# Split keys kept in DRAM between two passes, reciprocal sums transposed last, and a second score tile at first

## The chip, the cores and the metric

The kernel runs on one core of one Trainium2 chip. Its engines work side by side, each through a list of instructions of its own, in order: TensorE (PE, with its weight loads PEld), VectorE (DVE), ScalarE (ACT), GpSimd (POOL) and SyncE (SP), which here issues every DMA. The metric is the device time of one execution in microseconds, the median of several runs.

## The reference

Inputs are `q`, `k`, `v` (4 batches, 8 heads, 1152 positions, head size 64) and the weights `w_in` (512 x 2048) and `w_out` (2048 x 512); `q`, `k` and `v` come as float32, the weights as float64. Queries are averaged in pairs, so 576 of them meet 1152 keys:

```python
q_pool = q.reshape(B, H, S // factor, factor, D).mean(axis=3)      # factor = 2
scores = scale * np.matmul(q_pool, k.transpose(0, 1, 3, 2))        # scale = 1 / sqrt(D)
scores = scores - np.max(scores, axis=-1, keepdims=True)
attn = np.exp(scores)
attn = attn / (np.sum(attn, axis=-1, keepdims=True) + 1e-09)
attn_out = np.matmul(attn, v)
x = attn_out.transpose(0, 2, 1, 3).reshape(B * S // 2, H * D)      # 2304 x 512
h = x @ w_in
out = np.maximum(0.01 * h, h) @ w_out                              # 2304 x 512
```

## The kernel before

TensorE multiplies in a rounded float32 format (fp32r), so every operand is split into a rounded part ("hi") and the remainder ("lo"), and products are added up from hi and lo matmuls. Making the splits is work for ScalarE (the cast, hi), VectorE (the subtraction, lo) and GpSimd.

**Units.** Attention is cut into 64 units. A unit is one batch, one head and one of two groups of its 576 queries: group 0 has 256 queries in two tiles of 128, group 1 has 320 in three tiles of 108, 106 and 106. Batches 0 to 2 are worked in two passes: group 0 of all 8 heads, then group 1 of all 8 heads. Batch 3 takes both groups of a head in turn. Heads go in pairs that share a load of keys; a pair in a pass is a segment (`sg`), 28 in all.

**A unit's steps.** `load_q`, `q_sum` (GpSimd), `q_tr` (TensorE transpose) and `q_hi`, `q_lo` prepare the queries. For each pair of heads, `load_k` brings 576 KB of keys, `k_tr` transposes them in three groups of three (L311) into a `t` bank, and `k_hi` (cast on ScalarE) and `k_lo` (L326, subtraction on VectorE) write the split keys `kk`, one tile of 128 x 1152 per head, of which there are four. `qk` computes the scores of a query tile in two parts (L393 to L398) into the score banks, `vmax` (L406, L410) takes the row maximum on VectorE, `exp` (L420) the exponentials and their row sums on ScalarE. `rsum` (L429, L433) adds up the sums and takes reciprocals on VectorE; `r_tr` (L438) transposes them on TensorE, each broadcast over 128 columns, and `r_cp` copies them to `rb`. `tr` (L457) transposes the exponentials by key tile, `e_hi` and `e_lo` (L466) split them, `pvm` (L477) multiplies with the split values `vv`. `norm` adds hi and lo halves, multiplies by `rb`, and `x_out` stores the unit in DRAM.

**The feed-forward part.** The weights arrive as 32 tiles of 64-bit numbers and are converted to float32 by hand (`w_f32`: two VectorE, two ScalarE and one GpSimd instruction a tile, L520 to L536) and split (L545); the 16 tiles of `w_in` go to DRAM and are loaded again for each of nine blocks of 256 tokens (`l1`, L593: 192 matmuls a block; `l2`, L615 to L617: 96). A block can start when every head of its tokens is stored. The last three blocks hold tokens of batch 3 and need its last heads.

**What sets the order.** All instructions are issued in an order that a list scheduler makes when the program is built. A step has a priority (`prio`, by the number of its first query tile, smaller first), an estimated duration on its engine, steps that it needs, and buffers that it takes until other steps are done. At each turn, of the steps that could start earliest, the one with the smallest priority is issued. `AHEAD`, `SOONER`, `TR`, `SPLIT`, `PV`, `WIN`, `WOUT` and `WAHEAD` are constants in these priorities and in how many weight tiles are loaded ahead. The chip runs each engine's list in this order and waits on semaphores; the estimates only made the order.

**PSUM.** The eight banks of 512 columns are given out by name: one score tile `s` (banks 0 and 1) with its second part `s2` (2), three transpose banks `t` (3, 4, 7), one output bank `o` (5), one feed-forward bank `ml` (6). `tr` of a unit stands behind `r_tr` in the order that the scheduler may choose:

```python
tags["s"] = [(None, 0, slots("bank", (0, 1)))]
tags["t"] = [(None, 0, slots("bank", (3,), (4,), (7,)))]
tags["ml"] = [(None, 0, slots("bank", (6,))), ...]
step(tr, u, x, ..., order=[("r_tr", u)] if x == 0 else [("tr", u, x - 1)], ...)
```

## Time and profile before

| | |
|---|---|
| three runs | 1094.15, 1096.42, 1097.43 us; median 1096.42 |
| profiled execution | 1097.69 us, span on the core 1095.9 us |
| TensorE | 997.1 us busy (91%), 6748 matmuls; mean granted clock 0.970 |
| VectorE | 775.8 us (71%), 1625 instructions |
| ScalarE | 689.6 us (63%), 1693 |
| GpSimd | 406.2 us (37%), 402 |
| DMA | 158.55 MB, 145 GB/s mean, 43.8% of the 16 engines' time |

The span is the time from the first to the last instruction in the profiled execution. The busy share of an engine is a mean over stages that have different limits, so the table of the stages (below) says more than this one. A line such as L326 is the line of the kernel above. In a table of stretches, "PE 81.09 (x462)" is 81.09 us in which TensorE was busy, in 462 instructions that started there. Two matmuls overlap in the pipeline, so the time that one adds is the distance of the starts and not its own duration. The granted clock is a share of the full 2.4 GHz.

### The profile page before, as it was taken

The page shows a single profiled execution, that of the slowest core. Times are in us where ns is not written, and L with a number is a line of the kernel's source. Part 1 is how long each engine was busy: PE and PEld are TensorE (multiplying, and loading weights), DVE is VectorE, ACT ScalarE, POOL GpSimd, SP SyncE. Part 2 cuts the span into 40 slices and gives each one's busy share as a digit, 9 for nine tenths or more (in the row PEclk, how much of TensorE's full clock was granted, in tenths as well). Part 3 has the DMA queues.
Part 4 walks back from the last instruction along what each step waited for, and adds up shares of the span by engine and source line. Part 5 has one row for each costly group of instructions (what it writes and reads, how often), then busy time and mean ns, then how long its engine had stood idle before and what let it go on. Part 6 is the DMA issues. An engine that isn't in the chain of part 4 may idle for free.

```text
span 1095.9 us, 19300 instructions
## 1 busy us (share of the span) xinstructions
PE 997.1 (91%) x6748; PEld 906.3 (83%) x6748; DVE 775.8 (71%) x1625; ACT 689.6 (63%) x1693; POOL 406.2 (37%) x402
## 2 busy tenths in 40 slices
PE   5666788988999989999999999999999999799998
PEld 4555677787898979989899989988999888789896
DVE  7898889997788787777788788776778666411110
ACT  6777877877677666667677667776667665311110
POOL 5666557654233243222434242223222231133220
PEclk8788989999999999999999999999999999899999
DMA  8866546252264353524444433524243130286640
GB/s 263 283 213 214 179 141 232 84 210 90 73 203 143 103 161 100 170 79 150 144 157 134 136 129 116 182 66 162 76 136 105 30 125 25 63 293 231 191 164 29
DMA packets 83953, 158.55 MB, mean 145 GB/s; under 512 B 8592, under 2 KB 44944, under 8 KB 83856
## 3 DMA queue, kind: packets, MB, share of 16 engines
q1 hardware_dynamic: 83856, 157.32, 43.8%
q8 instruction: 53, 0.87, 0.3%
q14 instruction: 44, 0.36, 0.1%
HBM read 139.46 MB, written 17.83 MB: 144 GB/s over the span
## 4 chain that ended last, share of the span: by engine, by line
PE 68%; DVE 18%; issue 5%; DMA 4%; ACT 2%; POOL 2%; SPq 0%; DVEq 0%; POOLq 0%; ACTq 0%
PE banks L593 15%; PE banks L457 11%; PE banks L477 11%; PE banks L615 5%; PE banks L617 5%; PE banks L616 5%; DVE mx L406 5%; PE banks L393 4%; PE banks L394 4%; DVE kk L326 3%; DVE et L466 2%; PE banks L397 2%; PE banks L311 2%; PE banks L398 2%; DVE raw L529 2%
## 5 line engine op out<-in xcount | busy, mean ns | idle before, releaser
L466 DVE TENSOR_TENSOR et<-banks,et 128x320 fp32r<-128x320 f32 (+2 forms) x448 | 233.5, 536 | 70.3 <-ACT et L194 66.8
L194 ACT CAST et<-banks 128x320 fp32r<-128x320 f32 (+2 forms) x448 | 201.2, 470 | 120.5 <-PE banks L477 67.0
L406 DVE TENSOR_REDUCE mx<-banks 128x1 f32<-128x768 f32 (+2 forms) x320 | 234.2, 751 | 60.0 <-PE banks L394 49.9
L420 ACT ACTIVATE e<-banks,mx 128x768 f32<-128x768 f32 (+2 forms) x320 | 238.2, 745 | 56.6 <-DVE mx L410 49.8
L477 PE MATMUL banks<-et,vv 128*128 128x320 f32 (+1 forms) x1152 | 245.9, 323 | 5.8 <-DVE mx L410 4.1
L593 PE MATMUL banks<-xb,ws 128*128 128x256 f32 x1728 | 243.9, 286 | 7.8 <-ACT g L601 2.2
L457 PE MATMUL banks<-ident,e 128*128 128x128 f32 (+2 forms) x1440 | 219.2, 275 | 33.7 <-DVE et L466 14.5
L593 PEld LDWEIGHTS banks<-xb,ws 128*128 128x128 f32 x1728 | 224.2, 190 | 15.5 <-ACT g L601 4.8
L457 PEld LDWEIGHTS banks<-ident,e 128*128 128x128 f32 (+2 forms) x1440 | 174.9, 147 | 61.9 <-DVE et L466 21.6
L477 PEld LDWEIGHTS banks<-et,vv 128*128 128x128 f32 x1152 | 171.0, 194 | 10.8 <-DVE mx L410 5.0
L343 POOL TENSOR_TENSOR qs<-qn 80x256 f32<-80x256 f32 (+1 forms) x128 | 78.5, 633 | 195.8 <-PE banks L351 134.0
L606 POOL TENSOR_TENSOR gg<-g,gg 128x512 fp32r<-128x512 f32 x62 | 80.2, 1294 | 178.4 <-DVE gg L194 146.2
L393 PE MATMUL banks<-kk,qq 128*128 128x384 f32 (+2 forms) x320 | 118.1, 369 | 9.3 <-ACT e L420 9.1
L373 POOL TENSOR_TENSOR vv<-vr,vv 128x576 fp32r<-128x576 f32 x56 | 80.2, 1432 | 97.1 <-DVE vv L194 87.7
L394 PE MATMUL banks<-kk,qq 128*128 128x384 f32 (+2 forms) x320 | 111.4, 348 | 1.0 <-DVE qq L357 1.0
L326 DVE TENSOR_TENSOR kk<-banks,kk 64x384 fp32r<-64x384 f32 (+1 forms) x224 | 98.9, 454 | 14.2 <-ACT kk L194 10.0
L601 ACT ACTIVATE g<-banks 128x512 f32<-128x512 f32 x72 | 43.0, 597 | 102.2 <-PE banks L593 101.5
L615 PE MATMUL banks<-wo,gg 128*128 128x512 f32 x248 | 101.9, 411 | 0.9 <-ACT g L601 0.7
L194 ACT CAST kk<-banks 64x384 fp32r<-64x384 f32 (+1 forms) x224 | 83.9, 392 | 23.6 <-PE banks L311 13.7
L617 PE MATMUL banks<-wo,gg 128*128 128x512 f32 x248 | 97.6, 394 | 0.0
L616 PE MATMUL banks<-wo,gg 128*128 128x512 f32 x248 | 97.4, 393 | 0.0
L492 POOL TENSOR_TENSOR xo<-x,rb 64x256 f32<-64x256 f32 (+1 forms) x64 | 53.1, 829 | 71.4 <-DVE x L489 67.3
(60 smaller groups left out, 1275.1 us busy)
## 6 DMA issues: line engine op xcount, KB each, us to landing
ws<-wd SPq DMA_DIRECT2D x144, 512.0 KB, 4.3
vr<-in_v_dram SPq DMA_DIRECT2D x56, 288.0 KB, 3.4
kn<-in_k_dram SPq DMA_DIRECT2D x27, 576.0 KB, 3.9
raw<-in_moe_w_in_dram SPq DMA_DIRECT2D x16, 512.0 KB, 5.4
wd<-ws SPq DMA_DIRECT2D x16, 512.0 KB, 4.1
raw<-in_moe_w_out_dram SPq DMA_DIRECT2D x16, 512.0 KB, 5.0
qn<-in_q_dram SPq DMA_DIRECT2D x32, 160.0 KB, 2.4
out_dram<-raw SPq DMA_DIRECT2D x18, 256.0 KB, 2.0
```

What stands on the lines that cost most here:

```text
L194: ENG[e].copy(out=out, in_=in_) if e == "ACT" else ENG[e].tensor_copy(out=out, in_=in_)
L393: nc.tensor.matmul(p[:, c], lhsT=hi, rhs=key[:, c * CW:(c + 1) * CW], start=True, stop=False)
L394: nc.tensor.matmul(p[:, c], lhsT=lo, rhs=key[:, c * CW:(c + 1) * CW], start=False, stop=True)
L406: nc.vector.tensor_reduce(out=m[:, part:part + 1], in_=sps[u, j, part], axis=(AX.XY, AX.X)[part], op=ALU.max)
L420: nc.scalar.activation(out=d, in_=sps.pop((u, j, part)), func=AF.Exp, bias=mxs[u, j][:n, 2:3], accum_out=st[u][:n, c:c + 1])
L457: nc.tensor.transpose(p[:, a * w + o:a * w + o + n], ex[u, j][:n, t * 128:(t + 1) * 128], ident[:n, :n])
L466: nc.vector.tensor_tensor(out=et[u, x][:, 1, :w], in0=tps.pop((u, x))[:, :w], in1=f32(et[u, x])[:, 0, :w], op=ALU.subtract)
L477: nc.tensor.matmul(p, lhsT=vv[vis_of[u]][:, korder[vis_of[u] % 2][t], :], rhs=et[u, x][:, y, a * w:(a + 1) * w], start=(t == 0 and y == 0) ...
L593: nc.tensor.matmul(p, lhsT=wst[i, f][:, a, c, :], rhs=xx[i][:, x, c, :], start=(n == 0), stop=(n == 3 * KC - 1))
L615: nc.tensor.matmul(p, lhsT=gh, rhs=wo[f][:, 0], start=(f == hf * FH), stop=False)
L616: nc.tensor.matmul(p, lhsT=gh, rhs=wo[f][:, 1], start=False, stop=False)
L617: nc.tensor.matmul(p, lhsT=gl, rhs=wo[f][:, 0], start=False, stop=(f == hf * FH + FH - 1))
```

## The change

Three things change in what the steps do.

1. **Keys kept.** In batches 0 to 2 the first pass saves each head's split keys `kk` to a DRAM buffer (`k_save`, 128 x 1152 float32), and the second pass loads them into a `kk` tile (`k_back`) in place of `load_k`, `k_tr`, `k_hi` and `k_lo`. A `kk` tile of the first pass is free when both its last score matmul and its save are done.
2. **Reciprocal sums.** `r_tr` writes 64 rows from 64 broadcast columns instead of 128, its priority is `p0 + RT` (2.5) instead of `p0 - 1`, and `tr` no longer stands behind it.
3. **Banks.** Until the second part of the sixth unit's second tile has been exponentiated (`early`), banks 6 and 7 hold a second score tile; `ml` gets bank 6 and `t` bank 7 only after that.

Six constants differ too. (The new code also has a path for unsplit operands, `plain`, which is off with `PLAIN = 0` and left out here.)

```diff
+KEEP = True
+RT = 2.5
+EARLY = 5
-AHEAD = 3.0
-SOONER = 4.0
-TR, SPLIT, PV = 1.5, 1.0, 2.0
+AHEAD = 4.0
+SOONER = 5.0
+TR, SPLIT, PV = 1.5, 1.0, 3.0
-WAHEAD = 3
-WIN = (-2.0, 0.8)
-WOUT = (20.0, 1.0)
+WAHEAD = 2
+WIN = (0.0, 0.8)
+WOUT = (18.0, 1.0)
...
+    first_seg = {}
+    for sg, bh in enumerate(seg_bh):
+        first_seg.setdefault(bh, sg)
+    kept = {sg: first_seg[bh] for sg, bh in enumerate(seg_bh) if KEEP and PLAIN <= first_seg[bh] < sg}
...
+    kd = {2 * sg + j: dram.tile([128, S], F32, name=f"kd{2 * sg + j}") for sg in set(kept.values()) for j in range(2)}
...
-    tags["s"] = [(None, 0, slots("bank", (0, 1)))]
+    early = ("exp", EARLY, 1, 0)
+    tags["s"] = [(None, 0, slots("bank", (0, 1))), (None, early, slots("bank", (6, 7)))]
     tags["s2"] = [(None, 0, slots("bank", (2,)))]
-    tags["t"] = [(None, 0, slots("bank", (3,), (4,), (7,)))]
+    tags["t"] = [(None, 0, slots("bank", (3,), (4,))), (early, 0, slots("bank", (7,)))]
     tags["o"] = [(None, 0, slots("bank", (5,)))]
-    tags["ml"] = [(None, 0, slots("bank", (6,))), (tail, 0, slots("bank", (0,), (1,), (2,), (3,), (4,), (7,)))]
+    tags["ml"] = [(early, 0, slots("bank", (6,))), (tail, 0, slots("bank", (0,), (1,), (2,), (3,), (4,), (7,)))]
...
+    def k_save(hd, e):
+        nc.sync.dma_start(out=kd[hd], in_=f32(kk[hd]))
+
+    def k_back(hd, e, i):
+        kk[hd] = new("kk", i)
+        nc.sync.dma_start(out=f32(kk[hd]), in_=kd[2 * kept[hd // 2] + hd % 2])
...
-            nc.tensor.transpose(p[:, o:o + n], st[u][:n, 8 + j:9 + j].to_broadcast([n, 128]), ident[:n, :n])
+            nc.tensor.transpose(p[:64, o:o + n], st[u][:n, 8 + j:9 + j].to_broadcast([n, 64]), ident[:n, :n])
...
+            hold = [("qk", us[-1], len(tiles_of(us[-1])) - 1, 1)] + ([("k_save", hd)] if sg in kept.values() else [])
+            if sg in kept:
+                step(k_back, hd, prio=pr + 0.1, **sp(1, 0.59e6), deps=[("k_save", 2 * kept[sg] + j)],
+                     order=[("k_back", hd - 1) if j or sg - 1 in kept else ("k_tr", sg - 1, NCH - 1)], takes=[("kk", hold)])
...
+            if sg in kept.values():
+                gis = [gi for gi in range(NCH) if any(y[0] == j for y in KPART[gi])]
+                step(k_save, hd, prio=pr, **sp(1, 0.59e6), deps=[("k_lo", sg, gi, x) for gi in gis for x, y in enumerate(KPART[gi]) if y[0] == j])
...
+                if sg in kept:
+                    keys = [("k_back", hd)]
...
-        step(r_tr, u, prio=p0 - 1, eng=trs(*[x[1] for x in tiles_of(u)]), deps=[("rsum", u, 1)], takes=[("t", [("r_cp", u)])])
+        step(r_tr, u, prio=p0 + RT, eng=trs(*[64 for x in tiles_of(u)]), deps=[("rsum", u, 1)], takes=[("t", [("r_cp", u)])])
...
-                 deps=[("exp", u, t, x) for t in range(ntile) for x in range(2)], order=[("r_tr", u)] if x == 0 else [("tr", u, x - 1)], takes=[("t", [("e_lo", u, x)])])
+                 deps=[("exp", u, t, x) for t in range(ntile) for x in range(2)], order=[("tr", u, x - 1)] if x else [("r_tr", u)] if RT < 0 else [], takes=[("t", [("e_hi" if plain(u) else "e_lo", u, x)])])
```

What this does to the order of the instructions is seen at three places. In the changed kernel the score matmuls are L437 to L442, the key transposes L328, the query transposes L378, those of the exponentials L505 and of the sums L486, the value matmuls L531 and the second layer L674 to L676.

TensorE, the start. Before, from the second part of the first score tile on (`kk` and `qq` are the split keys and queries):

```order
L397 MATMUL banks<-kk,qq 128x384
L398 MATMUL banks<-kk,qq 128x384
L393 MATMUL banks<-kk,qq 128x384
L394 MATMUL banks<-kk,qq 128x384
L393 MATMUL banks<-kk,qq 128x384
L394 MATMUL banks<-kk,qq 128x384
L397 MATMUL banks<-kk,qq 128x384
L398 MATMUL banks<-kk,qq 128x384
L351 MATMUL banks<-ident,qs 128x128 x2
L311 MATMUL banks<-ident,kn 128x128 x9
```

Now, from the same matmul on:

```order
L441 MATMUL banks<-kk,qq 128x384
L442 MATMUL banks<-kk,qq 128x384
L437 MATMUL banks<-kk,qq 128x384
L438 MATMUL banks<-kk,qq 128x384
L437 MATMUL banks<-kk,qq 128x384
L438 MATMUL banks<-kk,qq 128x384
L328 MATMUL banks<-ident,kn 128x128 x6
L441 MATMUL banks<-kk,qq 128x384
L442 MATMUL banks<-kk,qq 128x384
L378 MATMUL banks<-ident,qs 128x128 x2
L328 MATMUL banks<-ident,kn 128x128 x3
```

Before, the whole second tile comes ahead of the next transposes of keys (`kn`). Now only its first part, which has banks 6 and 7, does; six key transposes stand between it and its second part.

TensorE, the sums of the 12th unit (batch 0, second pass). Before (`stat` holds the sums, `e` the exponentials, `wo` and `gg` belong to the second layer):

```order
L617 MATMUL banks<-wo,gg 128x512
L438 MATMUL banks<-ident,stat_67 128x108
L438 MATMUL banks<-ident,stat_67 128x106 x2
L393 MATMUL banks<-kk,qq 106x384
L394 MATMUL banks<-kk,qq 106x384
L393 MATMUL banks<-kk,qq 106x384
L394 MATMUL banks<-kk,qq 106x384
L457 MATMUL banks<-ident,e 128x108
L457 MATMUL banks<-ident,e 128x106 x2
L457 MATMUL banks<-ident,e 128x108
```

Now, around the same unit's sums:

```order
L676 MATMUL banks<-wo,gg 128x512
L674 MATMUL banks<-wo,gg 128x512
L675 MATMUL banks<-wo,gg 128x512
L676 MATMUL banks<-wo,gg 128x512
L486 MATMUL banks<-ident,stat_67 64x108
L486 MATMUL banks<-ident,stat_67 64x106 x2
L531 MATMUL banks<-et,vv 128x320 x4
L378 MATMUL banks<-ident,qs 128x80 x4
L531 MATMUL banks<-et,vv 128x320 x2
```

Before, the sums (L438) stand ahead of every transpose of the unit's exponentials. Now they stand behind the last of these, among the last value matmuls.

VectorE, from the 12th unit's sums on. Before (L326 makes the lo half of the keys, L466 that of the exponentials, L357 that of the queries):

```order
L429 SCALAR_TENSOR_TENSOR stat_67<-stat_67 108x3
L410 TENSOR_REDUCE mx<-mx 108x1
L433 RECIPROCAL stat_67<-stat_67 108x3
L194 CAST wo<-raw 128x512
L357 SCALAR_TENSOR_TENSOR qq<-banks,qq 128x320
L326 TENSOR_TENSOR kk<-banks,kk 64x384
L194 CAST wo<-raw 128x512
L326 TENSOR_TENSOR kk<-banks,kk 64x384
L406 TENSOR_REDUCE mx<-banks 106x1 x2
L466 TENSOR_TENSOR et<-banks,et 128x320
L410 TENSOR_REDUCE mx<-mx 106x1
```

Now (L514 is the lo half of the exponentials, L384 that of the queries, L453 and L457 are the maxima, L477 and L481 the sums and reciprocals, L584 and L588 convert weights):

```order
L477 SCALAR_TENSOR_TENSOR stat_67<-stat_67 108x3
L453 TENSOR_REDUCE mx<-banks 108x1
L481 RECIPROCAL stat_67<-stat_67 108x3
L457 TENSOR_REDUCE mx<-mx 108x1
L514 TENSOR_TENSOR et<-banks,et 128x320 x2
L384 SCALAR_TENSOR_TENSOR qq<-banks,qq 128x320
L584 TENSOR_SCALAR raw<-raw 128x512
L200 CAST wo<-raw 128x512
L588 SCALAR_TENSOR_TENSOR raw<-raw 128x512
L453 TENSOR_REDUCE mx<-banks 106x1 x2
L514 TENSOR_TENSOR et<-banks,et 128x320
L457 TENSOR_REDUCE mx<-mx 106x1
```

The key subtractions are gone from this stretch, which belongs to a second pass; subtractions of exponentials and a weight tile have moved up in their place.

On SyncE the 27 loads of 576 KB of keys become 15, and 24 saves and 24 loads back of 576 KB are added.

## Rows read from the trace of the kernel before

**Rows 1.** Busy time by stage: PE, PEld, DVE, ACT, POOL, clock, DMA share, GB/s.
```profile
0.00:20.00 20.00, 11.19 (x40) 8.69 (x40) 12.48 (x24) 13.39 (x29) 7.31 (x17) 1.00 0.80 252
20.00:140.00 120.00, 81.09 (x462) 69.59 (x462) 108.34 (x205) 90.73 (x209) 76.13 (x70) 0.83 0.66 221
140.00:260.00 120.00, 103.00 (x709) 91.61 (x709) 110.34 (x219) 93.29 (x228) 71.77 (x64) 0.97 0.49 166
260.00:920.00 660.00, 639.06 (x4524) 591.59 (x4525) 509.28 (x1108) 457.68 (x1158) 210.44 (x223) 0.99 0.38 122
920.00:960.00 40.00, 33.17 (x206) 29.26 (x205) 20.02 (x44) 17.76 (x43) 6.04 (x5) 0.87 0.18 54
960.00:1096.00 136.00, 129.64 (x812) 115.57 (x810) 15.36 (x31) 16.73 (x29) 34.51 (x25) 1.00 0.54 182
```

**Rows 2.** The profile's groups, VectorE: busy us, mean ns, idle before.
```profile
L326 DVE TENSOR_TENSOR kk<-banks,kk 64x384 fp32r<-64x384 f32 (+1 forms) x224 | 98.9, 454 | 14.2 <-ACT kk L194 10.0
```

**Rows 3.** Key subtractions (L326): stretch, length, DVE busy, clock, DMA share, GB/s.
```profile
140.00:260.00 120.00, 13.67 (x31) 0.97 0.49 166
```

**Rows 4.** Key transposes (L311): PE and PEld busy, else the same.
```profile
260.00:920.00 660.00, 26.00 (x171) 20.79 (x171) 0.99 0.38 122
```

**Rows 5.** TensorE in order of time: start, us, instruction, count, idle before.
```profile
215.32 0.49 PE L311 MATMUL banks<-ident,kn 128*128 128x128 f32 x3
215.56 0.54 PE L477 MATMUL banks<-et,vv 128*128 128x320 f32 x2
...
823.33 0.44 PE L351 MATMUL banks<-ident,qs 80*128 80x80 f32 x4
823.56 0.83 PE L477 MATMUL banks<-et,vv 128*128 128x320 f32 x4
...
834.40 0.82 PE L311 MATMUL banks<-ident,kn 128*128 128x128 f32 x6
834.98 0.42 PE L393 MATMUL banks<-kk,qq 128*128 128x384 f32 x1
```

**Rows 6.** Waits of TensorE, 260 to 920 us: total us, times, longest.
```profile
PE banks L438 <- DVE kk L326: 5.4, 5, 2.5
PE banks L457 <- DVE mx L410: 5.1, 5, 1.7
PE banks L457 <- DVE et L466: 3.4, 3, 1.6
...
PE banks L438 <- DVE stat L433: 1.2, 2, 1.0
```

**Rows 7.** The same, 0 to 140 us.
```profile
PE banks L457 <- DVE et L466: 9.6, 6, 4.1
...
PE banks L457 <- DVE mx L410: 5.1, 4, 1.4
...
PE banks L457 <- DVE kk L326: 3.0, 2, 2.4
```

**Rows 8.** TensorE in order of time, the start.
```profile
12.62 0.69 PE L393 MATMUL banks<-kk,qq 128*128 128x384 f32 x1 [2.49 <-ACT e L420]
...
22.78 0.69 PE L393 MATMUL banks<-kk,qq 128*128 128x384 f32 x1 [3.58 <-ACT e L420]
```

**Rows 9.** TensorE in order of time, the last unit.
```profile
940.59 0.80 PE L438 MATMUL banks<-ident,stat 108*128 108x108 f32 x3 [2.70 <-DVE stat L433]
```

**Rows 10.** DMA issues: count, KB each, median us to landing.
```profile
kn<-in_k_dram SPq DMA_DIRECT2D x27, 576.0 KB, 3.9
...
wd<-ws SPq DMA_DIRECT2D x16, 512.0 KB, 4.1
```

**Rows 11.** Transposes of the reciprocal sums (L438): columns as in rows 4.
```profile
140.00:260.00 120.00, 3.43 (x21) 2.00 (x21) 0.97 0.49 166
```

**Rows 12.** Weight loads of these: ns min/median/max, first and last start.
```profile
L438 PEld LDWEIGHTS banks<-ident,stat x160: 132/136/232, 25.7 to 940.8; 128*128 128x128 f32 x64, 106*128 106x128 f32 x64, 108*128 108x128 f32 x32
```

**Rows 13.** Waits of SyncE's queue: total us, times, longest.
```profile
SPq L300 <- PE banks L311: 68.2, 23, 11.5
```

More of the change, by code (lines that the diff above doesn't have):

```diff
@@ L361, in tile_pooled_attention_moe, with load_vv @@
     vn, vv = {}, {}
+    def load_vv(hd, e, i):
+        b, h = seg_bh[hd // 2]
+        vv[hd] = new("vv", i, F32).rearrange("p t d -> p (t d)")[:, :KT * D].rearrange("p (t d) -> p t d", t=KT)
+        nc.sync.dma_start(out=vv[hd], in_=v[b, h + hd % 2].rearrange("(p t) d -> p t d", t=KT))
     def load_v(hd, e, i):
@@ L388, in qk @@
         o, n = tiles_of(u)[j]
+        if plain(u):
+            head = units[u][4]
+            p = new(("s", "s2")[part], i)
+            p = sps[u, j, part] = p[:n, :128] if part else p[:n]
+            for c in [2] if part else [0, 1]:
+                half, first, m = ((head, 4 + 4 * head, 1) if part else ((head + c) % 2, (4 + c) * head, 4))
+                nc.tensor.matmul(
+                    p if part else p[:, c], lhsT=qq[u][64 * half:64 * half + 64, 0, o:o + n],
+                    rhs=kk[2 * units[u][3]][64 * half:64 * half + 64, 128 * first:128 * (first + m)], start=True, stop=True,
+                )
+            return
         key, hi, lo = kk[vis_of[u]], qq[u][:, 0, o:o + n], qq[u][:, 1, o:o + n]
@@ L475, in pvm @@
         for a, t in enumerate(kts(u)[x]):
+            if plain(u):
+                nc.tensor.matmul(
+                    p[0:64], lhsT=vv[vis_of[u]][:, (0, 2, 4, 6, 1, 3, 5, 7, 8)[t], :], rhs=et[u, x][:, 0, a * w:(a + 1) * w],
+                    start=(t == 0), stop=(t == KT - 1),
+                )
+                continue
             for y in range(2):
@@ L492, in norm, with norm_plain @@
             ENG[e].tensor_tensor(out=xos[u], in0=x1s.pop(u), in1=rbs.pop(u), op=ALU.mult)
+    def norm_plain(u, e, i):
+        w = width(u)
+        xos[u] = new("xo", i)[:, :w]
+        nc.vector.tensor_tensor(out=xos[u], in0=pv.pop(u)[0:64, :w], in1=rbs.pop(u), op=ALU.mult)
     def x_out(u, e):
@@ L634, in mm, with mm4 @@
         return {"PE": sum(0.0035 + 0.000445 * max(c, 240) for c in cols)}
+    def mm4(*cols):
+        return {"PE": sum(0.01 + 0.00182 * c for c in cols)}
     def trs(*rows):
@@ L663, in tile_pooled_attention_moe @@
         if u == us[0]:
-            if j == 0:
+            hold = [("qk", us[-1], len(tiles_of(us[-1])) - 1, 1)] + ([("k_save", hd)] if sg in kept.values() else [])
+            if sg in kept:
+                step(k_back, hd, prio=pr + 0.1, **sp(1, 0.59e6), deps=[("k_save", 2 * kept[sg] + j)],
+                     order=[("k_back", hd - 1) if j or sg - 1 in kept else ("k_tr", sg - 1, NCH - 1)], takes=[("kk", hold)])
+            elif j == 0:
                 for part in range(1 if sg else len(KLOAD)):
-                    before = ("load_k", sg, part - 1) if part else ("load_k", sg - 1, 0 if sg > 1 else len(KLOAD) - 1) if sg else None
+                    last = max([x for x in range(sg) if x not in kept], default=None)
+                    before = ("load_k", sg, part - 1) if part else ("load_k", last, 0 if last else len(KLOAD) - 1) if sg else None
                     step(load_k, sg, part, prio=pr - 4 + 0.01 * part - (0 if sg else 50), **sp(1, 0.59e6 if sg else 0.15e6), order=[before],
@@ L694, in tile_pooled_attention_moe @@
                 keys = [("k_lo", sg, gi, x) for x, y in enumerate(KPART[gi]) if y[0] == j]
[L695 removed]
+                if sg in kept:
+                    keys = [("k_back", hd)]
+                if plain(u):
+                    keys = [("k_cp", sg, gi)]
+                eng = mm4(swidth(u)[part]) if plain(u) else mm(*[CW] * (2 if part else 4))
+                step(qk, u, t, part, prio=n, eng=eng, deps=keys + [("q_hi" if plain(u) else "q_lo", u), ("qk", u, t, 0) if part else last],
                      takes=[("s2", [("exp", u, t, 1)]) if part else ("s", [("exp", u, t, 0)])])
[L697 to L698 removed]
+            step(vmax, u, t, 0, prio=n - SOONER, eng={"DVE": dve(2 * swidth(u)[0], psum=True)}, deps=[("qk", u, t, 0)], takes=[("mx", [("exp", u, t, 0), ("exp", u, t, 1)])])
+            step(vmax, u, t, 1, prio=n - SOONER, eng={"DVE": dve(swidth(u)[1], psum=True)}, deps=[("qk", u, t, 1)], order=[("vmax", u, t, 0)])
             step(vmax, u, t, 2, prio=n - SOONER, eng={"DVE": 0.15}, deps=[("vmax", u, t, 1), ("vmax", u, t, 0)])
```

63 lines of the change are left out of this document (44 added, 19 removed).

## The prediction

> **What bounds the kernel now.** I read the table by stages first, because the mean share of an engine hides three different limits. From 20 to 260 us VectorE is busy 108.34 and 110.34 of 120 us, 91%, and TensorE 81.09 and 103.00, 77% [rows 1]: VectorE sets the pace. From 260 to 920 us it is the other way: TensorE 639.06 of 660 us (97%), VectorE 509.28 (77%). From 920 to 960 us attention runs out and nothing is full (TensorE 33.17 of 40, granted clock 0.87); from 960 us on only the last three token blocks' matmuls are left, 129.64 of 136 us on TensorE. So a VectorE instruction removed before 260 us is worth its time, one removed after that is worth only the TensorE wait that it ends, and a TensorE instruction is the reverse.
>
> Next I read the groups of the operations that the change touches [rows 2 to 4], then single TensorE rows for what one transpose really costs in the stream [rows 5], and last the waits of TensorE in each stage [rows 6 to 9].
>
> **The keys of the second pass.** Batches 0 to 2 build the split keys of each of their 8 heads twice. The change keeps the first pass's result in DRAM: of 28 pairs of heads 12 lose 9 transposes, 8 VectorE subtractions and 8 ScalarE casts each, so 108 of 252 transposes and 96 of 224 subtractions go.
>
> VectorE: the 224 subtractions are busy 98.9 us, 0.442 each [rows 2]. Only those before 260 us count. Counted in VectorE's order, up to the row sums of the 16th unit (batch 0's second pass ends there) 73 subtractions stand before the change and 42 behind it, with all 32 weight tiles converted by then in both. The 31 that are gone agree with the trace, which has 31 of them in 140 to 260 us for 13.67 us [rows 3]. At full value that is 13.7 us. But TensorE is 86% busy in those 120 us and loses only some 30 transposes, so with 13.7 us less it would stand at about 94%; some of the gain will be lost there. I take 12; bounds 4 (TensorE takes over as the limit early) and 20 (VectorE, with fewer ScalarE casts ahead of its subtractions, also fills part of its 9% idle time).
>
> TensorE: 36 of the 108 transposes fall before 260 us, where they are covered by VectorE. The other 72 are in the stage that TensorE sets. Six of them take from 834.40 to 834.98, 97 ns each; three take from 215.32 to 215.56, 80 ns each [rows 5]. At 92 ns the 72 are worth 6.6 us. Upper bound by busy time: 171 transposes have 26.00 us in that stage [rows 4], 152 ns each, 10.9 us; lower bound 72 x 80 = 5.8.
>
> In the same stage TensorE waits 6.6 us at the transposes of the reciprocals (L438, behind VectorE's subtraction and the reciprocal itself) and 8.5 us at L457 for VectorE [rows 6]. 65 subtractions fewer in VectorE's queue and the moved transposes (next part) should end about half of these 15.1 us that touch L438 and a few at L457: I take 4; bounds 0 and 10.
>
> The added DMAs: 24 saves and 24 loads of 576 KB for 12 loads of the same size that go. Such a load takes 3.9 us to landing, a 512 KB write to DRAM 4.1 [rows 10]. A saved key has its whole first pass to land. In the order on SyncE each load back stands directly behind the query load of the unit before at the latest, and a unit of three tiles lasts some 17 us here (its three sums are transposed 21 times in the 120 us from 140 on, 7 units [rows 11]), so 4 us are covered by a unit's work. In 20 to 140 us the DMA engines are 66% busy [rows 1]; 8 saves are 4.7 MB, 21 us at the 221 GB/s of that stage, beside the other transfers. I take 1 us of loss; what late keys would cost is a rival below.
>
> **Reciprocals transposed last.** Before, the transposes of the exponentials (L457) may not be issued ahead of those of the unit's reciprocal sums (L438), which wait for two more VectorE steps. The last unit shows it plainly: TensorE sits 2.70 us until the reciprocal at 940.59, and only then starts on exponentials that were ready [rows 9]. Behind the change the exponentials go first and the sums come among the last matmuls of the unit; the normalisation waits for those matmuls anyway, so the later copy has cover. If that cover fails, the bank held for the sums keeps one transpose waiting for a copy of 0.4 us. Together with feed-forward matmuls that stand later (ahead of the second last unit's sums stand 1140 instead of 1152 of the first layer and 176 instead of 187 groups of the second, so work is left to fill gaps), I take 4 us of the stretch from 920 us; it holds 6.83 us of idle TensorE and runs at a clock of 0.87. Bounds 0 and 8.
>
> The transposes also get 64 stationary columns instead of 128. What sets their pace? The same 128 columns are loaded for the queries of 80 rows, and these follow each other at 58 ns (four from 823.33 to 823.56), against 80 to 97 ns for 128 rows [rows 5]: the pace goes with the moving rows, which stay. I take 0 for 160 transposes. The Trainium skill (TensorE: Matmul & The Clock Gate, LDWEIGHTS) says that a weight load takes its columns over 1.2 GHz, 107 ns for 128, whatever the rows; by it no transpose could follow another in under 107 ns and halving the columns would matter. The 58 ns above speak against that as the limit here. By the rule the sum would be 8.5 us better (160 x 53 ns); it is a rival below.
>
> **The second score tile.** In the first six units the scores of the next tile may be computed while the exponentials of this one still read their banks; the price is one of three transpose banks. At the start TensorE waits 2.49 and 3.58 us for ScalarE's exponential before a score matmul [rows 8]; with VectorE busy only 12.48 of the first 20 us [rows 1] these are worth something, later VectorE's weight conversion fills them. Bounds: a gain of 6.1 us, and a loss of 9.6, if the waits of L457 for VectorE in the first 140 us, 9.6 us in six, double with two banks [rows 7]. I take a gain of 3.
>
> The changed constants move work without adding any: in VectorE's order 15 instead of 18 weight tiles stand before the 8th unit's sums. VectorE does them later in the same VectorE-bound stage; nothing before 160 us needs them. I take 0.
>
> **Sum.** 12 + 6.6 + 4 + 4 + 3 - 1 = 28.6 us. The profiled execution took 1097.69 us (span 1095.9 and 1.8 around it), so 1069; the median of the runs is 1.3 lower, so **1068 us**.
>
> **Rivals.**
> *More than the terms.* The stage to 260 us closes fully (20), the start gains 6.1, the ends 8 and the waits 10: with 6.6 that is 51 us, 1046. For it: each stall of TensorE there is also one at a lower clock (0.83 in 20 to 140 us). Against: VectorE is at 91% and cannot give back more than its idle time. 14%.
> *Halved weight loads pay* on their own. The load's median is 136 ns [rows 12]; half of that, 160 times, is 10.9 us: 1057. Against: the 58 ns [rows 5]. 8%.
> *The freed VectorE time is not used*: up to 260 us ScalarE (78% of 140 to 260 us) or TensorE becomes the limit after 4 us, the two transpose banks eat the second tile's gain, and 6.6 + 4 + 4 remain with the loss of 1: 17.6 us, 1079; with the ends and waits at nothing too, 4 + 6.6 - 1, 1087, and with the 9.6 us of the banks on top 1096. For it: TensorE at 86%. 20%; a quarter of that lies within the measurement.
> *Late keys*, the case on the other side: SyncE issues in order and already waits 68.2 us at key loads for TensorE to free the tile [rows 13]; a load back waits for the last score matmul of a former owner. If it is issued too late TensorE stands for its whole landing, 3.9 us, up to 24 times. The gain of 28.6 is lost from 7 such stalls on; with half of the loads late, 12 x 3.9 = 47, the time is 1115. Against: the unit of lead above. 8%.
> *The forecast* has the remaining 50%, with its own range of 1056 to 1079.
>
> **Numbers.** Runs of this kernel tell apart about 0.3%, 3.3 us, so "faster" begins below 1093.1. Faster: 50 + 14 + 8 + 15 (three quarters of the unused time) = 87%. Same: 5 of that rival and 1 of the late keys, 6%. Slower: 7% of the late keys. The range reaches to the bigger gain at 1046 below and to the unused time's worst at the edge of no change above, 1092.
>
> **What would show it.** Right: the stage in which VectorE is over 90% busy ends some 12 us earlier, at the same count of converted weight tiles; VectorE's total falls by some 42 us (96 x 0.442) and TensorE's stage at 97% is shorter by about 10; no TensorE wait on a key load; the 2.70 us at the last unit are gone. Wrong: transposes at 64 columns that follow each other faster than 70 ns; a VectorE share well under 90% before 250 us with ScalarE or TensorE named as what it waits for; score matmuls (L437) waiting for a DMA; idle TensorE at the exponentials' transposes in the first 140 us above the 17.7 us of now (9.6 + 5.1 + 3.0) [rows 7].

## The result and the profile after

The changed kernel takes **1065.28 us** (median of four runs, 1062.37 to 1066.21), the kernel before 1095.29 beside it (1093.37 to 1097.43): a ratio of 0.9721, interval 0.9692 to 0.975. The profiled execution took 1066.17 us with a span of 1064.4, which is 31.5 less than before.

Busy time of each engine over the whole execution of the changed kernel, with its share and count:

```profile
PE 973.3 (91%) x6640; PEld 890.5 (84%) x6640; DVE 735.7 (69%) x1534; ACT 653.1 (61%) x1592; POOL 403.9 (38%) x402
```

TensorE lost 23.8 us of busy time (997.1 before), so of the 31.5 only 7.7 are idle time. The changed kernel by stage, columns as in [rows 1]:

```profile
0.00:20.00 20.00, 7.62 (x30) 5.99 (x31) 12.13 (x22) 11.71 (x25) 7.24 (x16) 0.83 0.90 298
20.00:140.00 120.00, 82.67 (x503) 71.16 (x503) 110.44 (x216) 92.25 (x214) 75.14 (x73) 0.86 0.82 270
140.00:260.00 120.00, 102.15 (x671) 93.53 (x671) 103.25 (x192) 80.47 (x197) 70.55 (x61) 0.92 0.51 170
260.00:920.00 660.00, 641.11 (x4556) 594.05 (x4555) 491.56 (x1071) 449.17 (x1124) 214.34 (x226) 1.00 0.45 144
920.00:960.00 40.00, 39.68 (x277) 36.86 (x276) 6.65 (x14) 7.55 (x14) 13.56 (x10) 1.00 0.71 232
960.00:1065.00 105.00, 100.09 (x612) 88.90 (x611) 11.69 (x23) 11.91 (x20) 23.03 (x17) 1.00 0.49 161
```

Against [rows 1], VectorE falls from 92% to 86% of 140 to 260 us and TensorE gains nothing there (102.15 against 103.00). The row from 920 us is full now (39.68 of 40), since attention has ended by then and only feed-forward matmuls are left.

Equal stretches of the clock hold different work, so I also cut both executions at the same work: where VectorE starts the row sums of the 17th unit (batch 0 is nearly through), and those of the 64th, the last. Before:

```profile
0.00:280.18 280.18, 215.15 (x1327) 187.16 (x1328) 246.81 (x480) 211.29 (x501) 158.76 (x152) 0.91 0.57 188
280.18:939.72 659.54, 634.93 (x4512) 587.56 (x4510) 506.94 (x1101) 455.74 (x1152) 207.89 (x222) 1.00 0.37 120
939.72:1095.90 156.18, 147.06 (x912) 131.59 (x912) 22.08 (x45) 22.55 (x41) 39.56 (x29) 0.97 0.51 170
```

After:

```profile
0.00:274.28 274.28, 204.65 (x1280) 181.26 (x1281) 238.17 (x455) 194.94 (x462) 157.26 (x154) 0.89 0.68 226
274.28:913.43 639.15, 622.34 (x4430) 577.56 (x4429) 475.58 (x1034) 435.97 (x1090) 207.62 (x220) 1.00 0.45 143
913.43:1064.40 150.97, 146.34 (x934) 131.66 (x932) 21.97 (x46) 22.15 (x41) 38.99 (x28) 1.00 0.54 176
```

The three stretches are shorter by 5.9, 20.4 and 5.2 us. The first-layer matmuls in them are 192, 960 and 576 in both kernels. Of the 288 groups of three matmuls of the second layer 25, 167 and 96 lie in them before, 21, 164 and 103 after. A group takes 0.7 us, so some 5 us of work have moved from the first two stretches into the last, and but for that the cuts compare like with like. One profile does not settle the first stretch: f3_128 below has the same order and no difference in time, and its stretches are 269.6, 638.8 and 152.3, so the first reads 5.9 or 10.6 us shorter. In both most of the gain is in the stage that TensorE sets; there TensorE is busy 12.6 us less (634.93 to 622.34) and idle 7.8 less.

The touched groups: key subtractions on VectorE in all (answers [rows 2]), then key transposes of 260 to 920 us ([rows 4]):

```profile
L343 DVE TENSOR_TENSOR kk<-banks,kk 64x384 fp32r<-64x384 f32 (+2 forms) x128 | 56.3, 453 | 13.4 <-ACT kk L200 11.2
```

```profile
260.00:920.00 660.00, 14.87 (x99) 11.98 (x99) 1.00 0.45 144
```

96 subtractions with 42.6 us and 72 transposes with 11.1 us of busy time are gone, as the counts said. TensorE's waits from 260 to 920 us ([rows 6]: total, times, longest):

```profile
PE banks L437 <- ACT e L468: 6.3, 9, 1.7
PE banks L505 <- DVE kk L343: 1.6, 3, 0.6
...
PE banks L505 <- DVE et L514: 1.5, 2, 1.0
PE banks L505 <- DVE mx L457: 1.3, 3, 0.9
```

No wait at the sums (L486) is in this view at all, and those at the exponentials' transposes fell from 9.0 to 4.4; score matmuls now wait 6.3 us for the exponential (0.5 before). At the end, TensorE in order of time ([rows 9]):

```profile
921.00 0.44 PE L486 MATMUL banks<-ident,stat 108*64 108x108 f32 x3
921.21 0.83 PE L531 MATMUL banks<-et,vv 128*128 128x320 f32 x4
```

The sums no longer have a wait in front. At the start, however ([rows 8]):

```profile
14.37 1.51 PE L328 MATMUL banks<-ident,kn 128*128 128x128 f32 x6 [3.26 <-DMA kn<-in_k_dram]
...
19.96 0.66 PE L378 MATMUL banks<-ident,qs 128*128 128x128 f32 x2 [3.45 <-DVE kk L343]
```

The two waits for the exponential (2.49 and 3.58) became one for a key load and one for VectorE, of 3.26 and 3.45. The first is for keys of a first pass, loaded from the input. The added transfers (count, KB, median us to landing):

```profile
kd<-kk SPq DMA_DIRECT2D x24, 576.0 KB, 4.9
kk<-kd SPq DMA_DIRECT2D x24, 576.0 KB, 4.6
```

No TensorE wait names `kk<-kd`.

### The profile page after: what moved, and what is told of

The parts are those of the page before. It is cut to its first block, busy times and chain, and to the rows that moved or that the text cites. A ratio compares the mean times of both kernels' runs of the same rounds, so it can differ in the third digit from the quotient of the medians.

```text
span 1064.4 us, 18999 instructions
## 1 busy us (share of the span) xinstructions
PE 973.3 (91%) x6640; PEld 890.5 (84%) x6640; DVE 735.7 (69%) x1534; ACT 653.1 (61%) x1592; POOL 403.9 (38%) x402
## 4 chain that ended last, share of the span: by engine, by line
PE 75%; DVE 14%; issue 4%; ACT 3%; DMA 2%; POOL 1%; SPq 1%; DVEq 0%; POOLq 0%; ACTq 0%
PE banks L652 17%; PE banks L531 12%; PE banks L505 12%; PE banks L674 6%; PE banks L676 5%; PE banks L675 5%; PE banks L437 5%; PE banks L438 5%; DVE mx L453 5%; PE banks L441 2%; PE banks L442 2%; DVE stat L477 2%; DVE kk L343 2%; DVE et L514 2%; PE banks L486 1%
## 5 line engine op out<-in xcount | busy, mean ns | idle before, releaser
L453 DVE TENSOR_REDUCE mx<-banks 128x1 f32<-128x768 f32 (+2 forms) x320 | 235.3, 753 | 75.7 <-PE banks L438 65.2
L200 ACT CAST et<-banks 128x320 fp32r<-128x320 f32 (+2 forms) x448 | 198.9, 471 | 123.2 <-PE banks L531 62.3
L514 DVE TENSOR_TENSOR et<-banks,et 128x320 fp32r<-128x320 f32 (+2 forms) x448 | 232.0, 535 | 56.4 <-ACT et L200 54.8
L652 PE MATMUL banks<-xb,ws 128*128 128x256 f32 x1728 | 247.0, 287 | 7.0 <-ACT g L660 2.2
L531 PE MATMUL banks<-et,vv 128*128 128x320 f32 (+1 forms) x1152 | 245.5, 321 | 1.5 <-DVE et L514 1.3
L652 PEld LDWEIGHTS banks<-xb,ws 128*128 128x128 f32 x1728 | 228.2, 192 | 14.7 <-ACT g L660 4.2
L505 PE MATMUL banks<-ident,e 128*128 128x128 f32 (+2 forms) x1440 | 209.5, 269 | 30.9 <-DVE et L514 13.3
L505 PEld LDWEIGHTS banks<-ident,e 128*128 128x128 f32 (+2 forms) x1440 | 169.7, 144 | 54.8 <-DVE et L514 20.2
L531 PEld LDWEIGHTS banks<-et,vv 128*128 128x128 f32 x1152 | 170.3, 192 | 5.2 <-DVE et L514 2.5
L665 POOL TENSOR_TENSOR gg<-g,gg 128x512 fp32r<-128x512 f32 x60 | 77.8, 1296 | 160.1 <-DVE gg L200 116.9
L370 POOL TENSOR_TENSOR qs<-qn 80x256 f32<-80x256 f32 (+1 forms) x128 | 74.9, 605 | 149.8 <-issue 80.2
L437 PE MATMUL banks<-kk,qq 128*128 128x384 f32 (+2 forms) x320 | 116.9, 365 | 12.8 <-ACT e L468 12.7
L438 PE MATMUL banks<-kk,qq 128*128 128x384 f32 (+2 forms) x320 | 111.3, 348 | 0.0
L674 PE MATMUL banks<-wo,gg 128*128 128x512 f32 x240 | 97.4, 406 | 1.5 <-DVE raw L684 0.8
L676 PE MATMUL banks<-wo,gg 128*128 128x512 f32 x240 | 94.6, 394 | 0.0
L675 PE MATMUL banks<-wo,gg 128*128 128x512 f32 x240 | 94.5, 394 | 0.0
L437 PEld LDWEIGHTS banks<-kk,qq 128*128 128x128 f32 (+2 forms) x320 | 59.3, 185 | 18.3 <-ACT e L468 16.9
L343 DVE TENSOR_TENSOR kk<-banks,kk 64x384 fp32r<-64x384 f32 (+2 forms) x128 | 56.3, 453 | 13.4 <-ACT kk L200 11.2
```

The costliest lines, as they stand in the source:

```text
L200: ENG[e].copy(out=out, in_=in_) if e == "ACT" else ENG[e].tensor_copy(out=out, in_=in_)
L437: nc.tensor.matmul(p[:, c], lhsT=hi, rhs=key[:, c * CW:(c + 1) * CW], start=True, stop=False)
L438: nc.tensor.matmul(p[:, c], lhsT=lo, rhs=key[:, c * CW:(c + 1) * CW], start=False, stop=True)
L453: nc.vector.tensor_reduce(out=m[:, part:part + 1], in_=sps[u, j, part], axis=(AX.XY, AX.X)[part], op=ALU.max)
L505: nc.tensor.transpose(p[:, a * w + o:a * w + o + n], ex[u, j][:n, t * 128:(t + 1) * 128], ident[:n, :n])
L514: nc.vector.tensor_tensor(out=et[u, x][:, 1, :w], in0=tps.pop((u, x))[:, :w], in1=f32(et[u, x])[:, 0, :w], op=ALU.subtract)
```

## The experiments

"Against the changed kernel" below means the difference of two ratios to the kernel before, times 1095.3 us. Each ratio is known to about 0.3%, so such a difference is known to some 4 us. In "frozen" kernels every instruction of the changed kernel keeps its place, and some are added, altered or left out; in the others the scheduler made the order anew.

### One suspected cost at a time, order frozen

**f1_dve** gives VectorE most of its removed time back: 144 maxima of 278 ns, six behind each load of kept keys.

```diff
     def k_back(hd, e, i):
...
+        for _ in range(6):
+            nc.vector.tensor_reduce(out=scr[:, 0:1], in_=ident[:64, :], axis=AX.X, op=ALU.max)
```

> Leaves the order of the changed kernel as it is and puts six VectorE maxima over 64x128 numbers of a constant, written to an unused word, behind each of the 24 loads back: 1.6 to 1.8 us of VectorE time a head in place of the 4 subtractions (1.77 us) that the change took away. The sum's theory: the 8 heads before 260 us cost their time (some 12 us), the 16 later ones about 4 through waits of TensorE; 1065 becomes 1077 to 1082. Rival, from the milestones of the two traces (the 16th unit's row sums come only 4.9 us earlier, and VectorE is busy 86% and no more 92% from 140 to 260 us): VectorE's freed time was mostly not used there; at most 5 us more, 1065 to 1070, and the gain must have come from TensorE's own instructions.

Measured: 1104.44 us, ratio 1.0066 (1.0042 to 1.0089), 37.8 us against the changed kernel. Both expectations missed. One of the 24 lumps, VectorE in order of time (in this kernel the line numbers there are three higher):

```profile
354.26 1.42 DVE L456 TENSOR_REDUCE mx<-banks 128x1 f32<-128x768 f32 x2 [0.45 <-PE banks L441]
355.59 1.83 DVE L356 TENSOR_REDUCE scr<-ident 64x1 f32<-64x128 f32 x6
357.35 0.67 DVE L517 TENSOR_TENSOR et<-banks,et 128x512 fp32r<-128x512 f32 x1
357.95 0.14 DVE L460 TENSOR_REDUCE mx<-mx 128x1 f32<-128x2 f32 x1
```

This lump stands between a tile's two row maxima and the small step that combines them; of the 24, two stand so and 19 between the first and the second maximum. The tile's exponential starts right after the combining step, at 358.12, so here the chain from scores to exponentials is held up by the whole lump. The 24 lumps last 1.83 us each, 44 in all, of which 37.8 are lost. Is it VectorE's time that costs, or that it comes in a lump?

**f1b_spread** adds the same 144 maxima singly, one behind each of six `e_lo` of every second-pass unit.

```diff
+        if units[u][3] in kept and 1 <= x <= 6:
+            nc.vector.tensor_reduce(out=scr[:, 0:1], in_=ident[:64, :], axis=AX.X, op=ALU.max)
```

> The order of the changed kernel with the same 144 VectorE maxima over 64x128 (278 ns each, 40 us in all) as in the run before with six in a lump, but spread: one behind each of six subtractions of exponentials in every unit of a second pass. New theory: VectorE's queue sets the pace in all of the attention, also where TensorE is busy 97% and VectorE 74%, because the order is tight (each result is made just when it is needed); the spread 40 us cost as much as the lumps, 1100 or more. Rival: it was the lump of 1.7 us that made TensorE miss one turn; spread into VectorE's gaps the 27 us behind 260 us cost little, 1075 to 1085.

Measured: 1068.85 us, ratio 0.9727 (0.9698 to 0.9755): 0.7 us, within the measurement and below both expectations. The singles last 38.6 us in all, but VectorE's busy time rises by only 22.2 here (757.9; 770.3 in f1_dve, 34.6 more), since they overlap partly with their neighbours. Of the 144, 48 stand inside the same chain, between a tile's first maximum and the combining step. So a delay of 0.28 us there is absorbed and one of 1.83 is not. The lumps differ from the singles in length and in place; no run has lumps outside the chain, so the two aren't told apart.

**f4_act**: eight ScalarE copies of 64x4 behind each load of kept keys.

```diff
+        for _ in range(8):
+            nc.scalar.copy(out=scr[:, 0:4], in_=ident[:64, 0:4])
```

> The order of the changed kernel with eight copies of 64x4 numbers on ScalarE behind each load back, about 1.6 us a head in place of the four casts (1.57 us) that the change took away. Theory that VectorE sets the pace: ScalarE (61% busy) has room, under 10 us, 1065 to 1075. Rival: casts, subtractions and transposes stand in one chain, and a lump on either engine costs alike, 1095 to 1104.

Measured: 1077.76 us, ratio 0.9809 (0.9781 to 0.9836), 9.6 us for 30.8 us more of busy ScalarE (683.9 in all), a third of it: between the two expectations, at the edge of the lower one.

**f2_pe** puts 108 transposes back on TensorE, four or five behind each load.

```diff
+        for _ in range(4 + hd % 2):
+            nc.tensor.transpose(banks[:, 2, 384:512], ident, ident)
```

> Leaves the order of the changed kernel as it is and puts back 108 TensorE transposes of 128x128 (of the identity, into columns of a score bank that nothing reads), 4 or 5 behind each load back. The sum's theory: the 72 in the stage that TensorE sets cost 92 ns each, the 36 before nothing: 6.6 us more, 1072. Rival (the trace's busy time of this line fell by 16.5 us): all of it counts, 153 ns each, 1082. Second rival: the gaps of TensorE take them, under 3 us.

Measured: 1073.16 us, ratio 0.9785 (0.9763 to 0.9808), 7.0 us. The starts of the units' row sums tell where: batch 0 loses nothing by them, batches 1 and 2 lose 4.7 and 4.0 us in the profiled execution. So the 72 of the TensorE-bound stage count, about 97 ns each, from a sum that is known to some 4 us.

**f3_128** broadcasts the sums over 128 columns again.

```diff
-            nc.tensor.transpose(p[:64, o:o + n], st[u][:n, 8 + j:9 + j].to_broadcast([n, 64]), ident[:n, :n])
+            nc.tensor.transpose(p[:, o:o + n], st[u][:n, 8 + j:9 + j].to_broadcast([n, 128]), ident[:n, :n])
```

> The changed kernel in the same order, with the reciprocal sums broadcast over 128 columns again instead of 64. The sum's theory: nothing, within 2 us of 1065, since the pace of transposes goes with the moving rows. Rival (halved weight loads pay): the weight load's median fell from 136 to 109 ns, 160 times 27 ns is 4.3 us, and 8.5 us by the rule of 1.2 GHz: 1070 to 1074.

Measured: 1066.29 us, ratio 0.9712 (0.969 to 0.9735), no difference. The weight loads (min/median/max ns), changed kernel and then this one:

```profile
L486 PEld LDWEIGHTS banks<-ident,stat x160: 105/109/176, 37.0 to 921.1; 128*64 128x64 f32 x64, 106*64 106x64 f32 x64, 108*64 108x64 f32 x32
```

```profile
L486 PEld LDWEIGHTS banks<-ident,stat x160: 132/136/232, 36.0 to 916.0; 128*128 128x128 f32 x64, 106*128 106x128 f32 x64, 108*128 108x128 f32 x32
```

Half the columns make a load 27 ns shorter, and the time doesn't notice. The Trainium skill (TensorE: Matmul & The Clock Gate, LDWEIGHTS) has the load's time proportional to its columns, which would have halved it; the trace shows a fifth. The starts tell why the time doesn't notice: after 260 us two transposes of the sums in a row start 108 ns apart (median) with 128 moving rows, at 64 columns and at 128 alike, and 94 and 93 ns with 106 rows.

**g2_max768** takes VectorE work away instead.

```diff
-        if part < 2:
-            nc.vector.tensor_reduce(
-                out=m[:, part:part + 1], in_=sps[u, j, part], axis=(AX.XY, AX.X)[part], op=ALU.max
-            )
-        else:
-            nc.vector.tensor_reduce(out=m[:, 2:3], in_=m[:, 0:2], axis=AX.X, op=ALU.max, negate=True)
+        if part == 0:
+            nc.vector.tensor_reduce(out=m[:, 2:3], in_=sps[u, j, part], axis=AX.XY, op=ALU.max, negate=True)
```

> The order of the changed kernel, with the row maximum taken over the first 768 of 1152 keys only (the shift in the exponent needs no exact maximum): 160 VectorE maxima over 384 columns (0.55 us) and 160 combining ones (0.145 us) are left out, 110 us of VectorE. Theory that VectorE sets the pace of attention: TensorE follows until its own work is the limit; the span falls by at least 50 us, to 1015 or less. Rival (TensorE sets the pace from 260 us on): only the stretch up to 260 us, a quarter of the units, gains, at most 28 us, and TensorE's 97% stay: 1037 to 1060.

Measured: 1054.09 us, ratio 0.96 (0.9571 to 0.9629). VectorE is busy 651.8 us, 84 less, and the time falls by 13.3, although the removed steps stand in the very chain that the lumps held up. The theory missed; the time lies within the rival's range, but the gain isn't where the rival put it. Up to the 17th unit VectorE is busy 18.8 us less (219.3 against 238.2) and the stretch takes 272.4 us, between the 269.6 and 274.3 of the two profiles with all maxima; the second stretch falls from 639.2 to 630.6. There TensorE goes from 97% to 98%:

```profile
260.00:920.00 660.00, 647.15 (x4618) 601.78 (x4616) 427.53 (x832) 448.31 (x1129) 217.70 (x229) 1.00 0.46 146
```

### One part of the change undone, order made anew

**c1_peek** is the gauge: the same work in another order.

```diff
-LAT = 0.12
+LAT = 0.13
```

> A gauge of the order alone: the changed kernel with the scheduler's estimate of the delay between engines at 0.13 in place of 0.12 us; every instruction is the same, only the order differs. Theory A (the parts have prices of their own): within 5 us of the changed kernel, 1060 to 1070. Theory B (any order made anew costs 10 to 20 us, since 0.12 suits this kernel by chance): 1075 to 1090.

Measured: 1069.7 us, ratio 0.9754 (0.973 to 0.9779): 3.6 us, within the measurement. So this new order moves little; the larger differences below are ten times that. It is one sample and no bound: r4_oldconst below is the same work in another order too, and moves 38.8.

**r1_nokeep** computes the keys twice again.

```diff
-KEEP = True
+KEEP = False
```

> The changed kernel without the kept keys: the second passes load, transpose and split them again; the order is made anew. The sum's theory: the keys were worth 12 + 6.6 + about 2 of the waits - 1, so some 20 us more, 1085. Rival (milestones): the keys were worth only their TensorE time and the rest came from the moved sums and the constants, 1072 to 1075.

Measured: 1102.33 us, ratio 1.0054 (1.0029 to 1.008): slower than before, and outside both expectations. In this company the kept keys are worth 36.5 us.

**r5_keeponly** has nothing but the kept keys and the 64 columns; beside this edit it takes the banks of r3_onetile and the constants of r4_oldconst, below.

```diff
-RT = 2.5
+RT = -1.0
```

> The kernel before with the kept keys and the 64 columns only: sums transposed first, one score tile, the old constants; the order is made anew. If the keys carry the whole gain, and the rest (6 us slower without them) is no help: 1065 or below. If the moved sums and the second tile add something once the keys are kept: 1070 to 1085.

Measured: 1113.29 us, ratio 1.0123 (1.0094 to 1.0153). Kept keys alone make the kernel slower, against both expectations. Its largest TensorE waits:

```profile
PE banks L486 <- DVE stat L481: 30.4, 18, 6.6
PE banks L437 <- ACT e L468: 17.8, 10, 3.9
```

**r2_rtfirst** moves only the sums back to the front.

```diff
-RT = 2.5
+RT = -1.0
```

> The changed kernel with the reciprocal sums transposed first again (RT = -1, and the exponentials' transposes stand behind them); kept keys, second score tile and constants as changed; the order is made anew. By the prediction's sum the moved sums are worth 4 us at the end and part of the 4 us of waits: 1069 to 1073. Theory A, the sums moved last are what lets the kept keys pay (kept keys without them and without the rest took 1113, with 30.4 us of TensorE waiting at the sums for VectorE): 1090 to 1115, with 20 us or more of idle TensorE in front of L486, most of it ended by VectorE's stat steps. Theory B, any order made anew moves the time by 10 to 20 us whatever is edited: the time is 1075 to 1090 and the idle time is spread over several lines.

Measured: 1117.3 us, ratio 1.0171 (1.0137 to 1.0205), 49.3 us against the changed kernel. The time fits theory A, but the sign that it named, 20 us of waits at L486 for VectorE, came out at 13.3 us. The bank shows more. A transpose of sums holds its bank until ScalarE has copied it to `rb`; there is one buffer `rb`, and it is free only when GpSimd has normalised the unit before. In order of time in this kernel, one unit's sums and their copy:

```profile
46.90 0.63 PE L486 MATMUL banks<-ident,stat 128*64 128x128 f32 x2 [0.93 <-DVE qq L384]
...
73.36 0.36 ACT L200 COPY rb<-banks 64x256 f32<-64x256 f32 x1 [1.76 <-POOL xo L546]
```

The bank is held for 26.8 us. In the kernel before, and in the changed one, at about the same time:

```profile
66.65 0.38 PE L438 MATMUL banks<-ident,stat 128*128 128x128 f32 x2
...
75.70 0.36 ACT L194 COPY rb<-banks 64x256 f32<-64x256 f32 x1 [0.16 <-POOL xo L492]
```

```profile
68.37 0.38 PE L486 MATMUL banks<-ident,stat 128*64 128x128 f32 x2
68.93 0.36 ACT L200 COPY rb<-banks 64x256 f32<-64x256 f32 x1
```

Paired this way over all 64 units, the sums hold a transpose bank for 159.8 us before (17 units over 3 us), 69.5 in the changed kernel (none over 3), 366.9 in r2_rtfirst and 220.4 in r5_keeponly. With two transpose banks in the first six units and one of them held, the exponentials' transposes have one. In r2_rtfirst:

```profile
59.31 1.11 PE L505 MATMUL banks<-ident,e 128*128 128x128 f32 x4 [1.98 <-DVE kk L343]
60.47 0.58 ACT L200 CAST et<-banks 128x512 fp32r<-128x512 f32 x1 [2.40 <-PE banks L505]
61.08 0.69 DVE L514 TENSOR_TENSOR et<-banks,et 128x512 fp32r<-128x512 f32 x1 [1.10 <-ACT et L200]
61.83 1.12 PE L505 MATMUL banks<-ident,e 128*128 128x128 f32 x4 [1.40 <-DVE et L514]
...
64.35 1.12 PE L505 MATMUL banks<-ident,e 128*128 128x128 f32 x4 [0.55 <-DVE et L514]
```

Transpose, cast, subtraction, next transpose: every group of four waits until the last has left its bank, 2.52 us a group. The Trainium skill (Perfetto Trace Analysis, Optimizing Tensor Performance) asks that independent matmul groups rotate through several banks so that emptying one overlaps with the next group; the trace shows 2.52 us a group where these transposes don't. From 20 to 100 us, this kernel and then the changed one:

```profile
20.00:100.00 80.00, 51.51 (x213) 41.90 (x213) 57.55 (x114) 48.53 (x110) 44.23 (x42) 0.61 0.72 247
```

```profile
20.00:100.00 80.00, 53.95 (x305) 45.94 (x305) 71.36 (x141) 60.77 (x141) 47.01 (x46) 0.81 0.82 277
```

213 matmuls take nearly the busy time of 305, at a mean granted clock of 0.61 instead of 0.81 (1.0 is the upper level, 2.4 GHz, and 0.5 the lower). Score matmuls start 0.32 us apart at 48 us in this kernel and 0.18 at 70 us in the changed one. The idle time is paid a second time in slower matmuls: over the whole execution the same 6640 matmuls keep TensorE busy for 1001.2 us instead of 973.3. How much of the 49.3 us the held bank causes isn't shown, since the order differs everywhere.

**r3_onetile** has the banks of before.

```diff
-    tags["s"] = [(None, 0, slots("bank", (0, 1))), (None, early, slots("bank", (6, 7)))]
+    tags["s"] = [(None, 0, slots("bank", (0, 1)))]
...
-    tags["t"] = [(None, 0, slots("bank", (3,), (4,))), (early, 0, slots("bank", (7,)))]
+    tags["t"] = [(None, 0, slots("bank", (3,), (4,), (7,)))]
```

> The changed kernel with the banks of before: one score tile, three transpose banks and the feed-forward bank from the start; all else as changed, order made anew. By the prediction's sum the second score tile is worth 3 us, bounds -9.6 to 6.1: 1068, from 1056 to 1071. Theory A (the sums moved last carry the gain): 1060 to 1072. Theory B (any order made anew costs 10 to 20 us): 1075 to 1090.

Measured: 1069.7 us, ratio 0.9748 (0.9715 to 0.978): 3.0 us, no more than the gauge.

**r4_oldconst** has the six constants of before.

```diff
-AHEAD = 4.0
-SOONER = 5.0
-TR, SPLIT, PV = 1.5, 1.0, 3.0
-WAHEAD = 2
-WIN = (0.0, 0.8)
-WOUT = (18.0, 1.0)
+AHEAD = 3.0
+SOONER = 4.0
+TR, SPLIT, PV = 1.5, 1.0, 2.0
+WAHEAD = 3
+WIN = (-2.0, 0.8)
+WOUT = (20.0, 1.0)
```

> The changed kernel with the six constants of before (AHEAD, SOONER, PV, WAHEAD, WIN, WOUT); all else as changed, order made anew. By the prediction's sum the constants are worth 0: 1062 to 1068. Theory A (the sums moved last carry the gain): the same, 1062 to 1072. Theory B (any order made anew costs 10 to 20 us): 1075 to 1090. A third possibility, the constants were what made the parts work together: 1085 to 1115.

Measured: 1104.5 us, ratio 1.0075 (1.0049 to 1.01), 38.8 us: the third possibility. The sums hold their bank for 70.4 us, so it isn't that. Its largest wait, over the whole execution, is no answer either, since c1_peek has 21.9 us of the same:

```profile
PE banks L505 <- DVE et L514: 19.4, 19, 3.3
```

By 160 us 26 weight tiles have passed their second VectorE step (L588) instead of 22, so VectorE has done more conversion ahead of attention. But c1_peek has 20 there and r1_nokeep 18, and only the second is slow, so the count alone doesn't explain it.

The stretches of above (us), the last four with the order frozen:

| kernel | to unit 17 | unit 17 to 64 | from there |
|---|---|---|---|
| before | 280.2 | 659.5 | 156.2 |
| changed | 274.3 | 639.2 | 151.0 |
| c1_peek | 276.6 | 641.7 | 149.5 |
| r3_onetile | 269.3 | 648.1 | 152.0 |
| r4_oldconst | 293.2 | 655.5 | 151.6 |
| r1_nokeep | 298.1 | 656.0 | 150.8 |
| r2_rtfirst | 299.1 | 660.2 | 155.8 |
| r5_keeponly | 293.1 | 663.3 | 149.8 |
| f3_128 | 269.6 | 638.8 | 152.3 |
| f1_dve | 288.1 | 662.5 | 152.4 |
| f1b_spread | 277.8 | 638.5 | 152.4 |
| g2_max768 | 272.4 | 630.6 | 152.5 |

Whichever of the keys, the sums or the constants is undone, 19 to 25 us go in the first stretch and 16 to 21 in the second. No version with a part undone beat the changed one by more than the measurement. None had its constants chosen anew for what was left, so whether one of them would do better with constants of its own is not tested.

## Why the prediction was right, and where its steps were not

The total was right (28.6 us forecast, 30.6 by the measured ratio), but in part by luck. By stretch, with the 1 us of the transfers put into the first, the forecast had 14 us up to the 17th unit (12 for VectorE, 3 for the score tile), 10.6 from there to the last unit and 4 behind it; the profile has 5.9 (10.6 in f3_128), 20.4 and 5.2. Too much in the first and too little in the second cancelled. By step:

- **72 key transposes, 6.6 us: right.** 7.0 when they were put back, within some 4. The spacing was misread, though: 97, 80 and 58 ns in [rows 5] divide in the short step to the next matmul. From one transpose to the next it is 109 ns with 128 rows and 69 with 80, and the next matmul of another kind starts 28 ns behind the last.
- **64 columns, nothing: right.** f3_128 refutes the rival of the halved weight loads, and the 69 ns at 128 columns still stand against the 107. The sign of being wrong, spacings under 70 ns, came out by that same division (two from 68.37 to 68.50) and means nothing, since the kernel before has 70 by it (66.65 to 66.79).
- **Transfers, 1 us, and the late keys: right that nothing waits for a key loaded back.** The 1 us was not measured by itself; the new wait of 3.26 us is for a key load of a first pass.
- **The second score tile, 3 us: not told apart.** r3_onetile has 3.0, the gauge 3.6. The waits of [rows 8] did go, but a key load and VectorE took their places.
- **The waits from 260 us on, 4 us: right in sign.** The 15.1 us at L438 and L457 became 4.4, and 6.3 at the score matmuls came in; all of TensorE's waits there sum to 21.3 us before and 18.0 after.
- **"VectorE sets the pace" before 260 us, 12 us: too high, and the reason is not borne out.** The first stretch is 5.9 to 10.6 us shorter. One reason is that the scheduler may place some casts on either engine and filled the freed time: up to the 17th unit 32 key subtractions (14.5 us) are gone from VectorE, but it got 14 casts of values and 12 of second-layer weights instead of 9 and 9, and its busy time fell only by 8.6 us. And a share of 91% was read as a limit, while g2_max768 takes 18.8 us of VectorE's time out of this stretch and it gets no shorter. Put back singly, 144 instructions cost 0.7 us in all; the first stretch of that profile (277.8) leaves open whether the 45 that stand there cost something. What limits there instead is not shown: the lumps point to the chain from scores through maxima to exponentials, with VectorE a link of it, but g2_max768 shortens that chain too. The rival of the unused time named this, but expected that it would show in the total.
- **The sums transposed last, 4 us: the mechanism was there, its size was not.** I priced the wait that shows, 2.70 us at the last unit [rows 9], and took the held bank for a copy of 0.4 us. The stretch from the last unit's row sums on did gain 5.2, with seven groups of the second layer more to do. But the bank was held for up to 9.4 us before, because the copy waits for the one `rb`, and undoing this part in the changed kernel costs 49.3.
- **The constants, nothing: wrong.** That they only move work was no reason for nothing: undone in the changed kernel they cost 38.8.

Beneath the two last points the form of the sum failed: it adds parts, and these don't add. Kept keys alone are 13.5 us slower than before (1.23%), the rest alone 5.9 slower (0.54%), both together 30.6 faster. The held banks go with the interplay of keys and sums: with the sums first, kept keys raise the hold from 159.8 to 220.4 us, with them last it is 69.5. They don't prove it, since in r5_keeponly TensorE also waits 30.4 us at the sums for VectorE's reciprocals (5.3 before), and r1_nokeep and r4_oldconst are as slow with the bank held for only 67.2 and 70.4 us. What the constants do in it stays open, and so does why the rest without the keys (r1_nokeep) is slower than before; there TensorE's largest wait is 17.1 us at the exponentials' transposes for VectorE's key subtractions, but no run separates that.

## What to carry to other kernels

An engine at 91% in a stage is not yet its limit: before it is priced, put its time back singly and in lumps and take some away, since here the same 144 instructions cost 0.7 or 37.8 us. Where a scheduler may place a step on either of two engines, count what it puts into the time that a change frees. Price an instruction that holds a buffer by how long it holds it, traced to the step that frees it, and not only by the wait that a profile prints. Where a scheduler makes the order, undo each part from the finished version as well as adding it to the old one; the two answers here differ in sign.
